# Fused attention and two-layer feed-forward on Trainium2: two more row tiles of w_out ahead of the second half of batch 1's x, and its transpositions in two groups

## The chip, the core and the metric

The kernel runs on one core of one Trainium2 chip. The metric is the device time of one execution in microseconds (us). The kernel before took 202.01 us, the median of 3 runs (201.93 to 202.19).

The engines are named as in the profile: PE (TensorE, matrix products), PEld (its weight loads), DVE (VectorE), ACT (ScalarE), POOL (GpSimd) and SP (SyncE, which here only issues DMAs). L1010 is line 1010 of the kernel.

## What is computed

Eight batches; each has eight heads of a 512 x 64 token matrix x and a 32 x 64 state. Both read each other by softmax attention, the two results are put one above the other (544 rows a batch), and the rows go through two layers with a leaky ReLU between them.

```python
B, H, S, Ns, D = (8, 8, 512, 32, 64)
scale = 1.0 / np.sqrt(D)
scores = scale * np.matmul(x, state.transpose(0, 1, 3, 2))
scores = scores - scores.max(-1, keepdims=True)
a = np.exp(scores)
a /= a.sum(-1, keepdims=True) + 1e-09
xread = np.matmul(a, state)
scores2 = scale * np.matmul(state, x.transpose(0, 1, 3, 2))
...
sread = np.matmul(a2, x)
attn_out = np.concatenate([xread, sread], axis=2)
x = attn_out.transpose(0, 2, 1, 3).reshape(B * S, H * D)
h = x @ w_in
g = np.maximum(0.01 * h, h)
return g @ w_out
```

## The kernel before

**Tiling.** Products take bf16 operands. w_in lies in SBUF as `w_in_bf` (4 blocks of 128 rows), w_out as `w_out_bf` (16 row tiles of 128 x 512). For each batch b an object `a0`, `a1`, `a2`, ... holds the attention's tiles. The first layer is folded with the state: `a_m` (L409) makes a quarter of M = state x w_in (8 small products into PSUM), `m_evict` (L429) copies it to SBUF, and `ff1` (L439) multiplies M by the probabilities `aT` into a bank named ph and applies the leaky ReLU on ACT into `hT`, one of 16 steps of 128 hidden units.

**Batch 0's second layer** is plain: `piece(b, hT, i, jq, js)` (L541) multiplies, for the token block i (four of 128 tokens), the hidden tiles 4 jq + js with the row tiles of w_out of the same numbers into a bank named py or pyw, one product of 128 x 512 each. `half` is `(range(0, 2), range(2, 4))`, so a piece with `half[0]` has two products.

**The order is written by hand**: each engine runs its instructions in the order of the program (`manual_schedule`, L51), and what an instruction waits for is put in as semaphores. The stretch that the change touches stands at L994 to L1037, between batch 0's first layer and batch 1's. In it, in the program's order:

- DVE casts the two halves of batch 1's x, `x1[0]` and `x1[1]` (heads 0 to 3 and 4 to 7, loaded as fp32), to bf16 tiles xb (L995), clears two columns of `stf` (L999), and SP issues eight small loads of the states of batches 2 and 3 into it (`load_state(0)`, L1000, L203).
- ACT makes batch 0's second softmax (`a_exp2`, L347). PE runs the pieces of the row tiles 0 and 1 (L1007, L1009).
- PE transposes batch 1's x by products with the identity, 8 for each half, into a PSUM tile pxt2 of the ring ph (L1015); DVE copies each to `a1.xT` (L1018). The profile prints pxt2 as pxt.
- PE runs the pieces of the row tiles 2 and 3 for token blocks 2 and 3 (L1020), then `a_scores(a1)` (L252: 8 products of the state with xT into sc) and `a_m(a1, 1)` with its copies on ACT (L1022), then the same row tiles for blocks 0 and 1 (L1024).
- DVE finishes batch 0's second softmax (`a_probs2`, L354), then batch 1's first: `a_shift` (row maxima L266, their spread L274, the difference L280) and `a_max2` (L341). POOL starts on sums of blocks of w_out, `tw_sum` (L577), which write over the buffers of x1 and xf.
- PE goes on with row tiles 4 to 7 (L1032), `a_m(a1, 2)` (L1033) and the rest of batch 0's second layer up to row tile 13 (L1036 to L1054). ACT takes the exponential (`a_exp`, L284), copies M (L1035), casts the two halves of batch 2's x (L1041) and makes `a_exp2(a1)` (L1044). SP transposes each half of batch 2's x by DMA (`a_xt_half`, L240). DVE closes the softmax (`a_recip`, `a_probs`: L289 to L302) with aT of batch 1.
- POOL scales the states of batches 2 and 3 (`state_cast(0)`, L209), SP transposes them by DMA into `st_t` (`state_t(0)`, L214) and loads batch 3's x (L1049).
- From L1066 on, `ff1(a1, h1, s)` and the last pieces of batch 0 run in turn; after step 4 come `a_scores(a2)` (L1077), which reads st_t and batch 2's xT.

**The loads** of weights and x up to batch 2 are issued by POOL at L871 to L885 in the order w_in (4), w_out rows 0-1, x1[0], x1[1], rows 2-3, rows 4-7, rows 8-11, first half of batch 2's x, rows 12-13, its second half, rows 14-15. They take eight semaphores in turn, so the ninth load waits on POOL until the first has landed, the tenth for the second, and so on.

Of the kernel before, what the change touches and what calls it, by code (L numbers as in the profile page):

```python
# [9 lines left out]
P = 128  # L10
B, H, S, D = 8, 8, 512, 64
# [4 lines left out]
NT = S // P  # L16
NK = H // 2
SCALE = 1.0 / (D ** 0.5)

BF16 = mybir.dt.bfloat16  # L20
# [7 lines left out]
def kernel(  # L28
# [9 lines left out]
    nc = tc.nc  # L38
# [8 lines left out]
    psum = ctx.enter_context(tc.tile_pool(name="psum", bufs=2, space=bass.MemoryType.PSUM))  # L47
# [5 lines left out]
    VEC, SCA, POO = nc.vector.tensor_copy, nc.scalar.copy, nc.gpsimd.tensor_copy  # L53
# [18 lines left out]
    ident = consts.tile([P, P], BF16, name="ident")  # L72
# [47 lines left out]
    def pair_of(a, t, k):  # L120
        h = 2 * (k % 2)
        return a.xb[k // 2][:, t, h:h + 2, :].rearrange("p h d -> p (h d)")
# [27 lines left out]
    def load_w_out_rows(j0, j1):  # L150
        nc.gpsimd.dma_start(
            w_out_bf[:, j0:j1, :], moe_w_out[P * j0:P * j1, :].rearrange("(j p) f -> p j f", p=P)
        )

    def load_w_out(c):
        load_w_out_rows(4 * c, 4 * (c + 1))
# [39 lines left out]
    stf = [consts.tile([P, hi - lo, P], FP32, name=f"stf{lo}") for lo, hi in groups]  # L196
    stb = [consts.tile([P, hi - lo, P], BF16, name=f"stb{lo}") for lo, hi in groups]

    def load_state(i):
        lo, hi = groups[i]  # L200
        for k in range(NK):
            for g in range(2):
                nc.sync.dma_start(  # L203
                    stf[i][NS * k:NS * (k + 1), :, D * g:D * (g + 1)],
                    state[lo:hi, 2 * k + g].rearrange("b n d -> n b d"),
                )
# [38 lines left out]
    def st_of(a, g, k):  # L245
        rows = slice(D * g, D * (g + 1))
        if a.b == 0:
            return stbd[rows, k, g ^ (k // 2), :]
        t = st1 if a.b == 1 else st_t[0][:, a.b - 2] if a.b < 4 else st_t[1][:, a.b - 4]
        return t[rows, NS * k:NS * (k + 1)]  # L250

    def a_scores(a):  # L252
        sc = psum.tile([P, 2, S], FP32, name="sc", tag="sc", bufs=1)
        for k in range(NK):
            for g in range(2):
                nc.tensor.matmul(  # L256
                    sc[NS * k:NS * (k + 1), g, :],
                    lhsT=st_of(a, g, k),
                    rhs=a.xTh[k // 2][D * g:D * (g + 1), :, k % 2, :],
                    start=True, stop=True,  # L260
                )
        a.sc = sc
# [52 lines left out]
    def a_shift(a):  # L315
        a_max(a)
        a_diff(a)
# [21 lines left out]
    def a_max2(a):  # L339
        a.m2 = att.tile([P, 2], FP32, name="mcol", tag="mcol")  # L340
        nc.vector.tensor_reduce(out=a.m2[:], in_=a.sc[:], axis=AX.X, op=ALU.max, negate=True)  # L341

    def a_exp2(a, g):
        if g == 0:
            a.e2 = att.tile([P, 2, S], BF16, name="e2", tag="e2")
            a.r2 = att.tile([P, 2], FP32, name="r2", tag="r2")
        nc.scalar.activation(  # L347
            out=a.e2[:, g], in_=a.sc[:, g, :], func=AF.Exp,
            bias=a.m2[:, g:g + 1], accum_out=a.r2[:, g:g + 1],
        )  # L350
# [3 lines left out]
    def a_probs2(a):  # L354
        nc.vector.tensor_scalar(out=a.r2[:], in0=a.r2[:], scalar1=1e-9, scalar2=None, op0=ALU.add)
        q2 = att.tile([P, 2], FP32, name="qc", tag="qc")
        nc.vector.reciprocal(q2[:], a.r2[:])
        if a.b in (0, 6):
            pairs[a.b] = att.tile([P, 2, 2, S], BF16, name="a2p", tag="a2p", bufs=1)
        if a.b in (0, 1, 6, 7):  # L360
            a.a2 = pairs[a.b - a.b % 2][:, a.b % 2]
        else:
            a.a2 = att.tile([P, 2, S], BF16, name="a2", tag="a2", bufs=1)[:]
        for g in range(2):
            nc.vector.tensor_scalar(
                out=a.a2[:, g, :], in0=a.e2[:, g, :],
                scalar1=q2[:, g:g + 1], scalar2=None, op0=ALU.mult,
            )
# [40 lines left out]
    def a_m(a, c, tag):  # L409
        if not hasattr(a, "M"):  # L410
            a.M = mpool.tile([P, 2, DFF], BF16, name="M", tag="M")
        if tag in ("ph", "py", "phpy"):
            pm = [psum.tile([P, DM], FP32, name="pm", tag=t) for t in (tag[:2], tag[-2:])]
            at = [t[:] for t in pm]
        else:
            pm = psum.tile([P, 2, DM], FP32, name="pm", tag=tag, bufs=1)
            at = [pm[:, g, :] for g in range(2)]
        for k in range(NK):
            for g in range(2):
                v, r = (k // 2, 2 * (k % 2) + (g ^ (k // 2))) if a.b == 0 else (g, k)  # L420
                nc.tensor.matmul(  # L421
                    at[v][NS * r:NS * (r + 1)],
                    lhsT=st_of(a, g, k),
                    rhs=w_in_bf[D * g:D * (g + 1), k, DM * c:DM * (c + 1)],
                    start=True, stop=True,
                )
        return pm

    def m_evict(a, c, pm, copy):  # L429
        cols = slice(DM * c, DM * (c + 1))  # L430
        if isinstance(pm, list):
            for g in range(2):
                copy(a.M[:, g, cols], pm[g][:])
        else:
            copy(a.M[:, :, cols], pm[:])  # L435
# [105 lines left out]
    def piece(b, hT, i, jq, bank=None, copy=SCA, js=range(4)):  # L541
        if jq == 0 and js[0] == 0:
            y = ys[b, i] = Y()
            y.py = psum.tile([P, DM], FP32, name="py", tag="py")[:] if bank is None else bank
        y = ys[b, i]
        for j in [4 * jq + v for v in js]:
            nc.tensor.matmul(  # L547
                y.py, lhsT=hT[:, j, P * i:P * (i + 1)], rhs=w_out_bf[:, j, :],
                start=(j == 0), stop=(j == 15),
            )  # L550
        if jq == 3 and copy is not None:
            y_store(b, i, copy)

    def y_store(b, i, copy):
        tag = ("ysb", "s1", "ysb", "s6")[i]
        ysb = ypool.tile([P, DM], FP32, name="ysb", tag=tag, bufs=3 if tag == "ysb" else 1)
        copy(ysb[:], ys[b, i].py)
        nc.sync.dma_start(rows_of(b)[i], ysb[:])
# [213 lines left out]
    a0, a1, a2 = att_of[:3]  # L772
# [102 lines left out]
    for u in range(2):  # L875
        nc.gpsimd.dma_start(
            x1[u][:], x[1, NK * u:NK * (u + 1)].rearrange("h (p t) d -> p h (t d)", t=NT)
        )
    load_w_out_rows(2, 4)
    load_w_out(1)  # L880
    load_w_out(2)
    load_x_half(2, 0)
    load_w_out_rows(12, 14)
# [52 lines left out]
    h0 = hpool.tile([P, 16, S], BF16, name="hT", tag="hT")  # L936

    def open_ff1_0(tag):
        if tag in ("sc", "big"):
            pr = psum.tile([P, 2, S], FP32, name="php", tag=tag, bufs=1)  # L940
            return pr, [pr[:, 0], pr[:, 1]]
        ph = [psum.tile([P, S], FP32, name="ph", tag=tag) for _ in range(2)]
        return ph, [p[:] for p in ph]
# [39 lines left out]
    for j, tag in ((4, "ph"), (6, "big"), (8, "py"), (10, "big"), (12, "py"), (14, "ph")):  # L983
        t, bk = open_ff1_0(tag)
# [5 lines left out]
        elif j == 8:  # L990
            a_scores(a0)
            m_halves(a0, 3, "ph")
            a_max2(a0)
    for u in range(2):  # L994
        VEC(  # L995
            a1.xb[u].rearrange("p t h d -> p h t d"),
            x1[u][:].rearrange("p h (t d) -> p h t d", t=NT),
        )
    nc.vector.memset(stf[0][:, 0, D - 1:D + 1], 0.0)  # L999
    load_state(0)  # L1000

    for g in range(2):
        a_exp2(a0, g)
    wide = psum.tile([P, 2, DM], FP32, name="pyw", tag="big", bufs=1)
    half = (range(0, 2), range(2, 4))
    for u in range(2):
        piece(0, h0, 2 + u, 0, bank=wide[:, u], js=half[0])  # L1007
    for i in (0, 1):
        piece(0, h0, i, 0, js=half[0])  # L1009
    for u in range(2):  # L1010
        ps = psum.tile([P, NT, 2, P], BF16, name="pxt2", tag="ph")
        for t in range(NT):
            for v in range(2):
                h = NK * u + 2 * v
                nc.tensor.transpose(  # L1015
                    ps[:, t, v, :], pair_of(a1, t, h // 2), ident[:]
                )
        VEC(a1.xT[:, :, 2 * u:2 * u + 2, :], ps[:])  # L1018
    for i in (2, 3):
        piece(0, h0, i, 0, js=half[1])  # L1020
    a_scores(a1)
    m_evict(a1, 1, a_m(a1, 1, "ph"), SCA)  # L1022
    for i in (0, 1):
        piece(0, h0, i, 0, js=half[1])  # L1024
    a_probs2(a0)
    a_shift(a1)
    a_max2(a1)
    tw_open()
    for j in (4, 6, 0, 2):
        tw_sum(1, j, j + 2, nc.gpsimd)  # L1030
    for i in (0, 1):
        piece(0, h0, i, 1)  # L1032
    pm = a_m(a1, 2, "ph")  # L1033
    a_exp(a1)
    m_evict(a1, 2, pm, SCA)  # L1035
# [93 lines left out]
    for b in range(2, B):  # L1129
# [22 lines left out]
        for s in range(16):  # L1152
# [75 lines left out]
            if b == 7 and s in FA_AT:  # L1228
                i = FA_AT.index(s)
# [49 lines left out]
    for n in (1, 2, 6, 5, 7, 3, 4):  # L1279
        two_product(q, n)  # L1280
        if n in (3, 4):
            u = n - 3
# [43 lines left out]
```

## Time and profile before

| | before |
|---|---|
| median of 3 runs | 202.01 us (201.93 to 202.19) |
| the profiled execution | 202.76 us |
| its span from first to last instruction | 201.0 us |
| granted clock of PE | 1.00 |
| PE busy, share of the span | 97% |
| DVE, ACT, POOL busy | 79%, 71%, 36% |

The profile and every view of the trace show that one profiled execution, with times from the start of its span. A timeline row gives the start, the duration, the engine, the line, the operation, what it writes and reads, and how many instructions are merged; in brackets stands the time the engine sat idle before it and what ended that. The chain of waits is the path that ended last, followed back from the end; its rows give start, duration, engine, tile and line.

### The profile page before, as it was taken

The page shows a single profiled execution, that of the slowest core. Times are in us where ns is not written, and L with a number is a line of the kernel's source. Part 1 is how long each engine was busy: PE and PEld are TensorE (multiplying, and loading weights), DVE is VectorE, ACT ScalarE, POOL GpSimd, SP SyncE. Part 2 cuts the span into 40 slices and gives each one's busy share as a digit, 9 for nine tenths or more (in the row PEclk, how much of TensorE's full clock was granted, in tenths as well). Part 3 has the DMA queues.
Part 4 walks back from the last instruction along what each step waited for, and adds up shares of the span by engine and source line. Part 5 has one row for each costly group of instructions (what it writes and reads, how often), then busy time and mean ns, then how long its engine had stood idle before and what let it go on. Part 6 is the DMA issues. An engine that isn't in the chain of part 4 may idle for free.

```text
span 201.0 us, 4628 instructions
## 1 busy us (share of the span) xinstructions
PE 195.4 (97%) x1880; PEld 130.1 (65%) x1880; DVE 158.7 (79%) x241; ACT 141.9 (71%) x274; POOL 72.6 (36%) x76
## 2 busy tenths in 40 slices
PE   7998999999999999999999999999999999999993
PEld 3643534443476767776776677676767777799982
DVE  3665799399999989985999889898999945984712
ACT  3678738899889868766887779777868555757420
POOL 8823272992091373037300760054004600540000
PEclk9999999999999999999999999999999999999999
DMA  6999998697999944852473404220025302210115
GB/s 198 207 207 297 212 290 147 119 346 170 196 219 228 308 49 72 237 216 55 88 225 139 128 16 92 104 109 0 0 104 157 58 0 104 108 49 8 52 38 170
DMA packets 38773, 27.75 MB, mean 138 GB/s; under 512 B 24416, under 2 KB 35808, under 8 KB 38752
## 3 DMA queue, kind: packets, MB, share of 16 engines
q1 hardware_dynamic: 33584, 20.78, 39.3%
q0 software_dynamic: 4832, 6.29, 15.4%
q10 hardware_dynamic: 336, 0.39, 0.8%
q8 instruction: 14, 0.23, 0.5%
q14 instruction: 7, 0.06, 0.1%
HBM read 17.30 MB, written 8.91 MB: 130 GB/s over the span
## 4 chain that ended last, share of the span: by engine, by line
PE 91%; DMA 3%; DVE 2%; ACT 1%; ACTq 1%; SPq 0%; issue 0%
PE ph L442 24%; PE ppx L642 18%; PE ppb L642 15%; PE py L547 7%; PE ppr L699 6%; PE pm L421 4%; PE pyw L547 3%; PE pf L520 3%; PE ppw L642 3%; DMA xf<-in_x_dram 2%; PE psr L394 2%; PE php L947 1%; PE ph L947 1%; PE sc L256 1%; DMA out_dram<-ysb 1%; DVE m L830 1%
## 5 line engine op out<-in xcount | busy, mean ns | idle before, releaser
L447 ACT ACTIVATE hT<-ph 128x512 bf16<-128x512 f32 x112 | 66.7, 605 | 25.2 <-PE ph L442 24.5
L442 PE MATMUL ph<-aT,M 128*128 128x512 bf16 x224 | 65.5, 380 | 0.0
L607 POOL TENSOR_TENSOR S<-hT,S 128x512 bf16<-128x512 bf16 x24 | 32.1, 1357 | 82.2 <-DVE S L607 55.5
L642 PEld LDWEIGHTS <-S 128*128 128x128 bf16 x384 | 37.0, 98 | 12.7 <-issue 0.9
L642 PEld LDWEIGHTS <-hT 128*128 128x128 bf16 x288 | 28.0, 98 | 11.1
L607 DVE TENSOR_TENSOR S<-hT 128x1024 bf16<-128x1024 bf16 x24 | 25.0, 1069 | 3.3 <-ACT hT L447 3.3
L442 PEld LDWEIGHTS <-M 128*128 128x128 bf16 x224 | 20.9, 98 | 8.8 <-issue 2.9
L642 PE MATMUL ppx<-tw,S 128*128 128x256 bf16 x160 | 20.8, 273 | 0.0
L547 PEld LDWEIGHTS <-hT 128*128 128x128 bf16 x96 | 9.1, 98 | 11.4 <-issue 1.0
L547 PE MATMUL py<-w_out_bf,hT 128*128 128x512 bf16 x64 | 16.0, 380 | 0.0
L739 DVE TENSOR_TENSOR ysb<-ppb,s 128x512 f32<-128x512 f32 x12 | 8.3, 692 | 6.2 <-PE ppb L642 6.1
L642 PE MATMUL ppb<-tw,S 128*128 128x256 bf16 x96 | 12.4, 273 | 0.0
L642 PE MATMUL ppb<-w_out_bf,hT 128*128 128x256 bf16 x96 | 12.4, 273 | 0.0
L642 PE MATMUL ppb<-w_out_bf,S 128*128 128x256 bf16 x96 | 12.3, 273 | 0.0
L435 ACT CAST M<-pm 128x1024 bf16<-128x1024 f32 x11 | 11.2, 1018 | 0.3 <-PE pm L421 0.3
L642 PE MATMUL ppx<-w_out_bf,hT 128*128 128x256 bf16 x80 | 11.2, 273 | 0.0
L347 ACT ACTIVATE e<-sc,mcol 128x512 bf16<-128x512 f32 x16 | 11.1, 700 | 0.0
L586 POOL TENSOR_TENSOR tw<-w_out_bf 128x512 bf16<-128x512 bf16 x8 | 9.0, 1153 | 4.2 <-DMA w_out_bf<-in_moe_w_out_dram 4.2
L642 PE MATMUL ppx<-tw,hT 128*128 128x256 bf16 x80 | 10.4, 273 | 0.0
L341 DVE TENSOR_REDUCE mcol<-sc 128x2 f32<-128x1024 f32 x8 | 9.7, 1214 | 0.0
L266 DVE TRANSPOSE_TENSOR_REDUCE mrow<-sc 128x32 f32<-128x1024 f32 x7 | 8.7, 1242 | 1.2 <-PE sc L256 1.2
L132 POOL CAST xb<-xl 128x2048 bf16<-128x2048 f32 x5 | 9.5, 1892 | 0.0
(148 smaller groups left out, 322.5 us busy)
## 6 DMA issues: line engine op xcount, KB each, us to landing
out_dram<-ysb SPq DMA_DIRECT2D x11, 512.0 KB, 2.6
xl<-in_x_dram SPq DMA_DIRECT2D x5, 1024.0 KB, 6.4
out_dram<-ysb SPq DMA_DIRECT2D x9, 256.0 KB, 4.7
w_in_bf<-in_moe_w_in_dram POOLq DMA_DIRECT2D x4, 512.0 KB, 9.8
xf<-in_x_dram SPq DMA_DIRECT2D x4, 256.0 KB, 3.7
w_out_bf<-in_moe_w_out_dram POOLq DMA_DIRECT2D x4, 256.0 KB, 13.6
x<-in_x_dram POOLq DMA_DIRECT2D x2, 512.0 KB, 14.6
w_out_bf<-in_moe_w_out_dram POOLq DMA_DIRECT2D x2, 512.0 KB, 16.5
```

The source lines that it names most:

```text
L132: nc.gpsimd.tensor_copy(xt[b][:].rearrange("p t h d -> p h t d"), xl[b][:].rearrange("p h (t d) -> p h t d", t=NT),)
L266: nc.vector.tensor_reduce(out=m1[:], in_=flat.rearrange("p (c j) -> p c j", j=NS), axis=AX.X, op=ALU.max, apply_transpose=True,)
L341: nc.vector.tensor_reduce(out=a.m2[:], in_=a.sc[:], axis=AX.X, op=ALU.max, negate=True)
L347: nc.scalar.activation(out=a.e2[:, g], in_=a.sc[:, g, :], func=AF.Exp, bias=a.m2[:, g:g + 1], accum_out=a.r2[:, g:g + 1],)
L435: copy(a.M[:, :, cols], pm[:])
L442: nc.tensor.matmul(ph[:], lhsT=a.M[:, g, P * j:P * (j + 1)], rhs=a.aT[:, g, :], start=(g == 0), stop=(g == 1),)
L447: nc.scalar.activation(out=hT[:, j, :], in_=ph[:], func=AF.Prelu, scale=1 / SCALE, alpha=0.01)
L547: nc.tensor.matmul(y.py, lhsT=hT[:, j, P * i:P * (i + 1)], rhs=w_out_bf[:, j, :], start=(j == 0), stop=(j == 15),)
L586: eng.tensor_tensor(out=tw[n][u][:, at], in0=in0, in1=in1, op=ALU.subtract)
L607: eng.tensor_tensor(out=part(n), in0=in0, in1=in1, op=op)
L642: nc.tensor.matmul(q[bank][v], lhsT=lhsT, rhs=w_of(n, j), start=q["open", bank] and j == 0, stop=j == 7, skip_group_check=True,)
L699: nc.tensor.matmul(q.bank[w], lhsT=lhsT, rhs=w_of(n, j), start=n in (1, 2, 5) and j == 0, stop=j == HJ - 1, skip_group_check=True,)
```

## The change

The loads of x1 and w_out are interleaved: row tiles 2-3 now stand ahead of x1[1], and the load of rows 4-7 becomes two, 4-5 and 6-7, of which both stand behind x1[1]. The casts, transpositions and copies of batch 1's x are done half by half: the first half as before; between its transpositions and those of the second half PE runs the pieces of row tiles 2 and 3 for all four token blocks. The second half's cast, `a_probs2(a0)` and its copy follow in this order on DVE. The pieces of row tiles 4 and 5 for blocks 0 and 1 now stand ahead of `a_scores(a1)`, those of 6 and 7 behind `a_m(a1, 1)`. The memset of stf and `load_state(0)` come behind the first copy.

```diff
@@ -876,8 +876,8 @@
         nc.gpsimd.dma_start(
             x1[u][:], x[1, NK * u:NK * (u + 1)].rearrange("h (p t) d -> p h (t d)", t=NT)
         )
-    load_w_out_rows(2, 4)
-    load_w_out(1)
+        load_w_out_rows(2 + 2 * u, 4 + 2 * u)
+    load_w_out_rows(6, 8)
     load_w_out(2)
     load_x_half(2, 0)
     load_w_out_rows(12, 14)
@@ -991,14 +991,26 @@
             a_scores(a0)
             m_halves(a0, 3, "ph")
             a_max2(a0)
-    for u in range(2):
+    def x1_cast(u):
         VEC(
             a1.xb[u].rearrange("p t h d -> p h t d"),
             x1[u][:].rearrange("p h (t d) -> p h t d", t=NT),
         )
-    nc.vector.memset(stf[0][:, 0, D - 1:D + 1], 0.0)
-    load_state(0)
-
+
+    def x1_t(u):
+        ps = psum.tile([P, NT, 2, P], BF16, name="pxt2", tag="ph")
+        for t in range(NT):
+            for v in range(2):
+                h = NK * u + 2 * v
+                nc.tensor.transpose(
+                    ps[:, t, v, :], pair_of(a1, t, h // 2), ident[:]
+                )
+        return ps
+
+    def x1_copy(u, ps):
+        VEC(a1.xT[:, :, 2 * u:2 * u + 2, :], ps[:])
+
+    x1_cast(0)
     for g in range(2):
         a_exp2(a0, g)
     wide = psum.tile([P, 2, DM], FP32, name="pyw", tag="big", bufs=1)
@@ -1007,29 +1019,25 @@
         piece(0, h0, 2 + u, 0, bank=wide[:, u], js=half[0])
     for i in (0, 1):
         piece(0, h0, i, 0, js=half[0])
-    for u in range(2):
-        ps = psum.tile([P, NT, 2, P], BF16, name="pxt2", tag="ph")
-        for t in range(NT):
-            for v in range(2):
-                h = NK * u + 2 * v
-                nc.tensor.transpose(
-                    ps[:, t, v, :], pair_of(a1, t, h // 2), ident[:]
-                )
-        VEC(a1.xT[:, :, 2 * u:2 * u + 2, :], ps[:])
-    for i in (2, 3):
+    x1_copy(0, x1_t(0))
+    nc.vector.memset(stf[0][:, 0, D - 1:D + 1], 0.0)
+    load_state(0)
+    x1_cast(1)
+    a_probs2(a0)
+    for i in (2, 3, 0, 1):
         piece(0, h0, i, 0, js=half[1])
+    x1_copy(1, x1_t(1))
+    for i in (0, 1):
+        piece(0, h0, i, 1, js=half[0])
     a_scores(a1)
     m_evict(a1, 1, a_m(a1, 1, "ph"), SCA)
-    for i in (0, 1):
-        piece(0, h0, i, 0, js=half[1])
-    a_probs2(a0)
     a_shift(a1)
     a_max2(a1)
     tw_open()
     for j in (4, 6, 0, 2):
         tw_sum(1, j, j + 2, nc.gpsimd)
     for i in (0, 1):
-        piece(0, h0, i, 1)
+        piece(0, h0, i, 1, js=half[1])
     pm = a_m(a1, 2, "ph")
     a_exp(a1)
     m_evict(a1, 2, pm, SCA)
```

## The prediction

> **What bounds the kernel now.** I read the page first, then the chain of waits, then each engine's timeline between 20 and 40 us. The page's shares of the chain that ended last:
>
> ```profile
> PE 91%; DMA 3%; DVE 2%; ACT 1%; ACTq 1%; SPq 0%; issue 0%
> ```
>
> PE is the path, so a change counts as far as it adds or takes away waits of PE. The chain of waits through the changed stretch, from batch 1's transpositions on (start, duration):
>
> ```profile
> 23.19 0.89 PE pxt L1015 x16
> 24.09 0.86 PE pyw L547 x4
> 24.95 0.47 PE sc L256 x8
> 25.41 0.22 PE pm L421 x8
> 25.63 2.69 PE py L547 x12
> 28.33 0.34 PE pm L421 x8
> 28.67 1.83 PE pyw L547 x8
> 30.50 1.73 PE py L547 x8
> 32.23 2.59 PE pyw L547 x12
> 34.82 0.86 PE py L547 x4
> ...
> 39.57 0.34 PE sc L256 x8
> 39.91 0.22 PE pm L421 x8
> ```
>
> All of it is PE, piece on piece. The one wait that I find is in the scores of batch 1: 0.47 us, where batch 2's, just as long and standing behind full products too, take 0.34. So **0.13 us** is all that this trace offers. The next views are the rows of DVE and, last, the first product of batch 1's first layer on PE:
>
> ```profile
> 21.27 0.69 DVE L995 CAST xb<-x 128x1024 bf16<-128x1024 f32 x1
> 22.52 0.69 DVE L995 CAST xb<-x 128x1024 bf16<-128x1024 f32 x1 [0.56 <-DMA x<-in_x_dram]
> ...
> 23.68 1.29 DVE L1018 COPY xT<-pxt 128x1024 bf16<-128x1024 bf16 x2 [0.45 <-PE pxt L1015]
> 24.88 0.16 DVE L355 TENSOR_SCALAR r<-r 128x2 f32<-128x2 f32 x1
> ...
> 25.28 0.62 DVE L365 TENSOR_SCALAR a2p<-e,qc 128x512 bf16<-128x512 bf16 x2
> 25.81 1.24 DVE L266 TRANSPOSE_TENSOR_REDUCE mrow<-sc 128x32 f32<-128x1024 f32 x1
> ...
> 33.87 0.69 DVE L302 TENSOR_TENSOR aT<-e,qb 128x1024 bf16<-128x1024 bf16 x1
> ...
> 39.98 1.25 DVE L266 TRANSPOSE_TENSOR_REDUCE mrow<-sc 128x32 f32<-128x1024 f32 x1 [1.22 <-PE sc L256]
> ```
> ```profile
> 35.52 1.03 PE L442 MATMUL ph<-aT,M 128*128 128x512 bf16 x4
> ```
>
> DVE is a chain of its own here: from the row maxima (25.81) to the end of aT (33.87 + 0.69 = 34.56) it is 8.75 us, one operation behind the other. PE takes up aT at 35.52, so this chain has 0.96 us in hand.
>
> **PE's own work.** The number of products does not change. After the change, from 23.19 on, with the rows above: 8 transpositions (half of 0.89) to 23.64; 8 products of row tiles 2 and 3 (2 x 0.86) to 25.36; 8 transpositions to 25.81; 4 products of row tiles 4 and 5 to 26.67; scores without a wait, 0.34, to 27.01; a_m 0.22 to 27.23; 4 products 0.86, and 0.10 more behind small products (the 12 take 2.69, three times 0.86 is 2.58), to 28.19; a_m 0.34 to 28.53; then 1.83 + 1.73 + 2.59 + 0.86 = 7.01 to 35.54. Before, that point is 35.68. By work alone PE would gain 0.14.
>
> The operands are there. The casts' row shows x1[1] landing at 22.52; loads run in order, and from the landing of rows 2-3 below one load is about 1.1, so it lands at 23.6. DVE takes it up only behind the first copy (half of 1.29 from 23.68, to 24.4), ends the cast at 25.1 and a_probs2 (24.88 to 25.90 now, 1.02) at 26.1. PE's second transpositions start at 25.36, after the cast. The second copy then ends near 26.7, where PE wants it: nothing, at most 0.1.
>
> **A new wait on ACT.** The change leaves 4 products between the two a_m, where there were 12. The two banks of the ring ph must be copied out between:
>
> ```profile
> 25.67 1.07 ACT L433 CAST M<-pm 128x512 bf16<-128x512 f32 x2 [1.59 <-PE pm L421]
> ...
> 29.62 1.06 ACT L284 ACTIVATE e<-sh 128x1024 bf16<-128x1024 f32 x1 [2.88 <-DVE sh L280]
> ...
> 31.52 1.06 ACT L126 CAST xb<-xl 128x1024 bf16<-128x1024 f32 x1
> 33.41 1.04 ACT L126 CAST xb<-xl 128x1024 bf16<-128x1024 f32 x1 [0.83 <-DMA xl<-in_x_dram]
> ```
>
> The copies end 1.11 after a_m (26.74 against 25.63), so at 28.34; PE comes at 28.19. That is 0.15 to 0.2, and PE reaches batch 1's first layer at 35.5 to 35.7, about as before.
>
> **The softmax starts later.** This decides. Before, the scores ended at 25.41, and DVE took them up at 25.81, when a_probs2 was done. Now they end at 27.01; batch 2's maxima start 0.07 after their scores (39.91 to 39.98), so these start at 27.08, **1.27 later**. The exponential on ACT lies beside batch 1's second maximum on DVE, so nothing in the 8.75 us gives way: aT ends at 35.83. With some 0.05 for the hand-over the first layer starts at 35.88 instead of 35.52: **+0.36 us**, in which the gain and the ACT wait above are swallowed. Everything that PE does later moves with it.
>
> **Behind the exponential.** Its start (29.62) moves by the same 1.27, and with it ACT's M copies and the cast of batch 2's first half. SP waits for that cast:
>
> ```profile
> 23.27 3.63 SPq L203 DMA_DIRECT2D stf<-in_state_dram  x8
> ```
> ```profile
> 32.60 2.05 SPq L240 DMA_TRANSPOSE xT<-xb  x1
> ```
> ```profile
> 34.76 1.24 SPq L240 DMA_TRANSPOSE xT<-xb  x1
> 36.10 1.19 SPq L214 DMA_TRANSPOSE st_t<-stb  x1
> ```
> ```profile
> st_t<-stb SPq DMA_TRANSPOSE x1, 2.9
> ```
> ```profile
> 39.49 0.11 PEld L256 LDWEIGHTS <-st_t 64*32 64x32 bf16 x8 [0.42 <-DMA st_t<-stb]
> ```
> ```profile
> L372 SPq DMA_TRANSPOSE a2T<-a x4: 1232/1270/2805, 54.4 to 110.8; - x4
> ```
>
> The first cast ends at 32.58 and SP issues at 32.60, so now at 33.87. The second cast, which waited for its load at 33.41, now runs from 33.85 to 34.9 and is no later than its turn on SP. With the durations of these rows (2.16 to the next issue, 1.34 to the one behind it) st_t is issued at 37.37 and lands 2.9 later, at 40.3; before, 36.10 + 2.9 = 39.0. PE loads it at 39.49 now and would come at 39.85: a **second wait of about 0.45 us**, to 40.3. What is uncertain is the issue of 2.05: the next one, as large, took 1.24, and the row of a2T, also as large, spans 1.23 to 2.81. With 1.24, st_t lands at 39.5 and the wait is gone; with 2.81 it grows by 0.76. I take 2.05, since it is the same instruction's own row.
>
> The eight loads of stf start behind the first copy, at 24.4 instead of 23.27, and their 3.63 us end at 28.1, well ahead of 33.87. The scaling on POOL, which waits for them, then has until 37.37. Batch 3's x, behind st_t on SP, moves by 1.27 as well; I cost it at nothing, since its first products come in b = 2, and at up to 0.9 (1.27 less 0.36) if that cover is gone. POOL's tw sums can start earlier, as row tiles 4 and 5 land sooner; nothing but batch 2's products reads them.
>
> Sum: 0.36 + 0.45 = 0.81 us against the profiled execution (span 201.0, time 202.76). I add it to the median, 202.01, as it stands: **202.8 us**.
>
> **The rivals.**
>
> *Only the first wait*: the issue of xT takes 1.24 to 1.6. 202.01 + 0.36 = 202.4, on the bound of what a measurement can tell from no change (0.2%, 0.4 us). For it: the second xT issue took 1.24, and half of the a2T row 1.27 or less. Against it: the instruction's own 2.05. A long one, 2.81, makes 203.6.
>
> *The loads are later in the timed runs than in the profiled one, and the sum ends at no change or below.* The place is PE's first use of x1[1] and of row tiles 2 and 3. The POOL rows and two times to landing:
>
> ```profile
> 8.31 0.75 POOL L151 DMA_DIRECT2D w_out_bf<-in_moe_w_out_dram  x1
> ...
> 12.40 0.74 POOL L151 DMA_DIRECT2D w_out_bf<-in_moe_w_out_dram  x1 [1.77 <-DMA w_in_bf<-in_moe_w_in_dram]
> 16.10 0.76 POOL L106 DMA_DIRECT2D xl<-in_x_dram  x1 [2.96 <-DMA w_in_bf<-in_moe_w_in_dram]
> ```
> ```profile
> w_out_bf<-in_moe_w_out_dram POOLq DMA_DIRECT2D x1, 256.0 KB, 15.3
> ```
> ```profile
> w_out_bf<-in_moe_w_out_dram POOLq DMA_DIRECT2D x1, 512.0 KB, 16.7
> ```
>
> Rows 2-3 land at 8.31 + 15.3 = 23.6 and are used at about 24; the second cast ends at 23.21 and its transpositions start near 23.5. So before has only some 0.2 to 0.3 in hand. After the change it is 0.8: x1[1] at 23.6 against 24.4 on DVE, and row tiles 4 and 5 (23.6 + 1.3) against 25.81. If the loads are late by L, before loses L - 0.2 and the changed kernel nothing up to 0.8, so the change wins back at most 0.6: 201.8 if st_t does not wait, 202.2 if it does. It decides from L = 0.56 on. For it: the timed runs are 0.75 us shorter than the profiled one. Against it: PE has no wait for a load in this stretch.
>
> *The split load holds up all the loads behind it.* POOL waits for the eighth load before, so with one load more, rows 8-11 go out at 16.10, in the slot of the next load, not at 12.40. If a load always took its 16.7 us, they would land at 32.8 instead of 29.1; PE wants them at 30.5, waits 2.3 us and reaches the first layer at 37.8: 202.01 + 2.2 = 204.2. Against it: x1[1] and rows 2-3, issued in turn, land 1.1 us apart, each after 15 us, so the time is spent in a queue that stays full, and a later place in POOL's order does not move a landing. The Trainium skill ("DMA: Bandwidth & Descriptors", section "Anatomy of one DMA — SWDGE (gpsimd) path") gives each such DMA a fixed cost of about 2.0 us, mostly its completion, beside its bytes; added to every load behind, rows 8-11 would come at an estimated 31.1 and the sum would be near 203. The spacing of 1.1 us, under that fixed cost, speaks against adding it.
>
> *Neither wait comes*: if DVE's chain were 0.36 shorter and st_t in time, PE keeps its 0.14, 201.9. No row of the chain shows a gap to close.
>
> **How the numbers follow.** Both waits as priced, 0.42: slower. Only the first, 0.26, divided by the bound: 0.09 slower, 0.17 the same. A longer issue, 0.05: slower. Late loads, 0.18: 0.11 the same, 0.07 faster (where the last rival comes with it: 201.9 - 0.6 = 201.3). The split, 0.04: slower. Neither wait, 0.05: 0.03 the same, 0.02 faster. That is slower 0.60, the same 0.31, faster 0.09. The range of 201.8 to 203.2 takes in the first two cases and most of the late loads and leaves out 203.6, 204.2 and the faster end, 0.18 in all.
>
> **What would show it.** In the changed trace: the row maxima of batch 1 near 27.1, aT ending near 35.8, PE's first ph<-aT,M at 35.9 behind a gap of 0.2 to 0.5; the xT issue on SP near 33.9; the weight load of st_t near 40.3 behind a wait for its DMA; the second a_m of batch 1 behind ACT. Landings of rows 8-11 and of batch 2's x unmoved. It is wrong if the maxima start before 26.5, if st_t lands before 39.9 (then 202.4), or if a wait of PE for a load that the profile hides was there before.

## The result, and the profile after

The changed kernel took **204.84 us** (median of 6 runs), the kernel before, on the same chip, 202.22 us (6 runs). One disturbed run of the changed kernel (207.36 us) is left out of the ratio; the median of the five others is 204.30. The ratio is 1.012, with a 95% interval of 1.0083 to 1.0157: slower by 1.7 to 3.2 us, where the forecast was 202.8 and its range ended at 203.2. The profiled execution took 205.61 us with a span of 203.8, against 201.0 before, and the granted clock was 1.00 in both, so the two traces can be laid side by side. It is the longest of the five (204.14 to 205.61), so what its trace shows as lost lies above the 2.4 us of the ratio.

The shares of the chain that ended last, from the page of the changed kernel:

```profile
PE 74%; DVE 16%; ACT 3%; DMA 3%; issue 2%; ACTq 1%
```

Before, it was PE 91% and DVE 2%. Where DVE came onto the path is seen in the chain of waits of the changed kernel, from batch 1's transpositions on (start, duration):

```profile
23.11 0.46 PE pxt L1005 x8
...
23.60 0.69 DVE xT L1011
...
24.82 1.13 DVE r L355
...
26.17 2.16 DVE a2p L365 x2
...
28.33 0.61 DVE xT L1011
...
28.98 0.42 PE sc L256 x4
...
29.43 1.26 DVE mrow L266
...
37.50 0.70 DVE aT L302
38.20 0.05 issue
38.24 0.62 PE ph L442 x2
```

The chain leaves PE at 23.60 and comes back to it for good only at 38.24, with the first product of batch 1's first layer. The waits of PE between 20 and 60 us, all of them (who waited, for whom, us in total, times, the longest):

```profile
PE sc L256 <- DVE xT L1011: 2.1, 1, 2.1
PE py L547 <- issue: 0.2, 1, 0.2
```

So PE waits in the scores of batch 1 for the second copy of xT, which I had costed at nothing, at most 0.1. None of its waits is for a load or for st_t. DVE's timeline shows why the copy is late:

```profile
24.21 0.69 DVE L995 CAST xb<-x 128x1024 bf16<-128x1024 f32 x1
...
24.82 1.12 DVE L355 TENSOR_SCALAR r<-r 128x2 f32<-128x2 f32 x1
25.97 0.17 DVE L357 RECIPROCAL qc<-r 128x2 f32<-128x2 f32 x1
26.17 2.16 DVE L365 TENSOR_SCALAR a2p<-e,qc 128x512 bf16<-128x512 bf16 x2
28.25 0.68 DVE L1011 COPY xT<-pxt 128x1024 bf16<-128x1024 bf16 x1
29.43 1.25 DVE L266 TRANSPOSE_TENSOR_REDUCE mrow<-sc 128x32 f32<-128x1024 f32 x1 [0.50 <-PE sc L256]
```

No row of a_probs2 has a bracket: DVE waits for nothing there. But the same instructions have become longer. The 128x2 L355 takes 1.12 instead of 0.16, the two L365 2.16 instead of 0.62, a_probs2 as a whole 3.5 instead of 1.0. The reciprocal between them still takes 0.17. What else had changed at that time stands in POOL's timeline; before:

```profile
26.29 4.50 POOL L586 TENSOR_TENSOR tw<-w_out_bf 128x512 bf16<-128x512 bf16 x4 [4.18 <-DMA w_out_bf<-in_moe_w_out_dram]
```

and after, where the first, the second with the third, and the fourth of these sums are shown apart:

```profile
24.23 1.68 POOL L586 TENSOR_TENSOR tw<-w_out_bf 128x512 bf16<-128x512 bf16 x1 [1.67 <-DMA w_out_bf<-in_moe_w_out_dram]
...
25.88 2.30 POOL L586 TENSOR_TENSOR tw<-w_out_bf 128x512 bf16<-128x512 bf16 x2
...
28.14 1.20 POOL L586 TENSOR_TENSOR tw<-w_out_bf 128x512 bf16<-128x512 bf16 x1
```

The first sum reads row tiles 4 and 5 and waits for their load. Before, that load brought 4 to 7, and the sum started at 26.29, behind a_probs2 (which ended at 25.28 + 0.62 = 25.90). Now it starts 2.06 us earlier, at 24.23, ahead of a_probs2. And the ends agree: the first sum ends at 24.23 + 1.68 = 25.91 and L355 at 24.82 + 1.12 = 25.94; the third ends at 25.88 + 2.30 = 28.18 and the second L365 at 26.17 + 2.16 = 28.33.

**Theory 1.** A DVE operation of certain kinds that reads SBUF (tensor_scalar and cast among them) and a POOL sum that reads SBUF do not run beside each other: the one that comes second stands still until the first is done, and the time is put down to it as duration. L355 and the two L365 each stand behind a sum that was there first. The second copy, behind them in DVE's order, PE's scores, the maxima and the softmax chain are late by that.

**The rivals**: the two engines share a bandwidth, so that each gets slower in proportion to what it moves; the new order of PE, or the later start of the softmax, costs the time and the long L355 and L365 only fill a wait; the new order of the loads costs it, by what then lands late.

### The profile page after: what moved, and what is told of

The parts are those of the page before. It is cut to its first block, busy times and chain, and to the rows that moved or that the text cites. A ratio compares the mean times of both kernels' runs of the same rounds, so it can differ in the third digit from the quotient of the medians.

```text
span 203.8 us, 4603 instructions
## 1 busy us (share of the span) xinstructions
PE 195.1 (96%) x1853; PEld 130.8 (64%) x1880; DVE 161.6 (79%) x241; ACT 142.0 (70%) x274; POOL 73.6 (36%) x77
## 4 chain that ended last, share of the span: by engine, by line
PE 74%; DVE 16%; ACT 3%; DMA 3%; issue 2%; ACTq 1%
PE ph L442 18%; PE ppx L642 18%; PE ppb L642 15%; PE ppr L699 5%; PE pf L520 3%; PE pm L421 3%; PE ppw L642 3%; PE ph L947 2%; DVE sh L274 2%; PE psr L394 2%; DVE mrow L266 2%; DMA xf<-in_x_dram 2%; DVE a2p L365 1%; DVE qb L298 1%; DVE r L289 1%
## 5 line engine op out<-in xcount | busy, mean ns | idle before, releaser
L442 PE MATMUL ph<-aT,M 128*128 128x512 bf16 x202 | 60.9, 379 | 0.2
L642 PE MATMUL ppb<-w_out_bf,S 128*128 128x256 bf16 x96 | 12.3, 273 | 0.1
L586 POOL TENSOR_TENSOR tw<-w_out_bf 128x512 bf16<-128x512 bf16 x8 | 9.6, 1228 | 1.7 <-DMA w_out_bf<-in_moe_w_out_dram 1.7
```

Source lines behind the costliest of these rows:

```text
L442: nc.tensor.matmul(ph[:], lhsT=a.M[:, g, P * j:P * (j + 1)], rhs=a.aT[:, g, :], start=(g == 0), stop=(g == 1),)
L586: eng.tensor_tensor(out=tw[n][u][:, at], in0=in0, in1=in1, op=ALU.subtract)
L642: nc.tensor.matmul(q[bank][v], lhsT=lhsT, rhs=w_of(n, j), start=q["open", bank] and j == 0, stop=j == 7, skip_group_check=True,)
```

## The experiments

The traces differ by about 1 us in when batch 1's transpositions start: 22.18 to 23.03 us in the kernel before and those made from it, 22.44 to 23.24 in the changed one and those made from it. So in each profiled run I count from PE's first transposition of batch 1 (pxt): to the first product ph<-aT,M of batch 1's first layer, and to the end of the span. Before, these are 35.52 - 23.03 = 12.49 and 201.0 - 23.03 = 177.97. The table gives what is added to them, and the measured ratio to the kernel before, which was run beside it. The ratio comes from all the runs, the last two columns from one profiled run each.

| kernel | median, us (runs) | ratio, 95% interval | first layer | end |
|---|---|---|---|---|
| changed kernel | 204.84 (6) | 1.012, 1.0083 to 1.0157 | +2.80 | +2.88 |
| e1: changed, POOL held | 202.72 (12) | 1.0024, 1.0013 to 1.0035 | +0.39 | +0.49 |
| e2: before, new loads alone | 204.20 (4) | 1.009, 1.0077 to 1.0103 | +2.06 | +2.15 |
| e3: changed, old loads | 203.66 (5) | 1.0059, 1.0046 to 1.0072 | +0.55 | +0.69 |
| e4: changed, a_probs2 later | 203.79 (6) | 1.0087, 1.0061 to 1.0114 | +0.40 | +1.48 |
| e5: before, three more sums on POOL | 203.44 (9) | 1.0065, 1.0043 to 1.0088 | +1.34 | +1.49 |
| e7: changed, L365's scalings on ACT | 202.97 (12) | 1.0035, 1.0009 to 1.0061 | +1.59 | +1.69 |
| e8: changed, POOL's sums halved | 204.18 (7) | 1.0071, 1.004 to 1.0102 | +1.36 | +1.45 |
| e9: before, PE's two groups alone | 203.57 (6) | 1.0057, 1.0038 to 1.0075 | +1.16 | +1.23 |
| e10: e9, POOL held | 202.76 (12) | 1.0019, 1.0006 to 1.0033 | -0.09 | +0.08 |
| e11: before, POOL held | 202.18 (11) | 0.9995, 0.9983 to 1.0008 | 0.00 | -0.01 |

### e1: POOL held back in the changed kernel

A small copy on POOL reads batch 1's row maxima, so the sums behind it start when a_probs2 is long done. All else is the change.

```diff
+    held = att.tile([P, NB], FP32, name="held", tag="held", bufs=1)
+    nc.gpsimd.tensor_copy(held[:], a1.m1[:])
     for j in (4, 6, 0, 2):
         tw_sum(1, j, j + 2, nc.gpsimd)
```

> The changed kernel, with POOL's first sums of w_out held back until batch 1's row maxima are done (a 128 x 32 copy on POOL that reads them stands ahead of the sums). Theory 1 (POOL's sums, which now start at 24.2 us, hold up DVE's a_probs2): a_probs2 takes 1.0 us again instead of 3.5, the row maxima start near 27.1, the first layer of batch 1 near 35.9, and the time is 0.3 to 0.9 us over before. Rival A (the split load and the slots of the load queue make the loads late) and rival B (the order of PE's work alone): the row maxima stay near 29.4 and the time 2 to 3 us over before.

DVE's rows and POOL's:

```profile
24.31 0.16 DVE L355 TENSOR_SCALAR r<-r 128x2 f32<-128x2 f32 x1
...
24.70 0.61 DVE L365 TENSOR_SCALAR a2p<-e,qc 128x512 bf16<-128x512 bf16 x2
...
26.50 1.25 DVE L266 TRANSPOSE_TENSOR_REDUCE mrow<-sc 128x32 f32<-128x1024 f32 x1 [0.55 <-PE sc L256]
```
```profile
28.06 4.50 POOL L586 TENSOR_TENSOR tw<-w_out_bf 128x512 bf16<-128x512 bf16 x4
```

a_probs2 is back at 1.0 us. The maxima come 26.50 - 22.44 = 4.06 behind the first transposition (6.48 in the changed kernel), and of +2.80 at the first layer +0.39 is left. The ratio goes down from 1.012 to 1.0024, by some 1.9 us. Most of the loss is the collision; what is left is the size of the first wait that I had forecast.

### e2 and e3: the loads alone, the order alone

e2 is the kernel before with the first hunk of the change only:

```diff
-    load_w_out_rows(2, 4)
-    load_w_out(1)
+        load_w_out_rows(2 + 2 * u, 4 + 2 * u)
+    load_w_out_rows(6, 8)
```

> The kernel before, with the new order of the loads alone. Theory 1: POOL's sums start near 24.2 instead of 26.3, while DVE is at a_probs2 (24.9 to 25.9), which grows by 1.5 to 2.5 us; the row maxima start near 28, and since aT has 0.96 us in hand, the time is 0.7 to 1.8 us over before. Rival A: 2 us or more over before, with a wait of PE for a load. Rival B: within 0.5 us of before, with the row maxima at most 1 us later, since x1's second half lands 1 us later.

```profile
25.12 0.35 DVE L355 TENSOR_SCALAR r<-r 128x2 f32<-128x2 f32 x1
...
25.72 2.28 DVE L365 TENSOR_SCALAR a2p<-e,qc 128x512 bf16<-128x512 bf16 x2
```
```profile
24.30 4.71 POOL L586 TENSOR_TENSOR tw<-w_out_bf 128x512 bf16<-128x512 bf16 x4 [1.66 <-DMA w_out_bf<-in_moe_w_out_dram]
```

The loads alone bring the collision: the sums start at 24.30, a_probs2 takes 2.9. PE also waits 1.07 at its second group of transpositions, whose x lands later now and, without the new order, is wanted at once. The maxima come 27.92 - 22.18 = 5.74 behind the first transposition instead of 2.78: of these 2.96 us, 1.9 are a_probs2 and 1.1 the later x, which by itself would have used up little more than the 0.96 in hand. 1.009 (+1.8 us) is at the upper end of what theory 1 had expected.

e3 is the changed kernel with that hunk taken back.

> The changed kernel, with the loads as before. Theory 1: rows 4-7 land near 26.1, so the sums start when a_probs2 is over and it stays at 1.0 us; PE waits some 0.4 us for these rows ahead of the scores, the maxima start near 27.5, and the time is 0.5 to 1.3 us over before. Rival A: no slower than before by over 0.4. Rival B: 2 to 3 us over before.

```profile
25.50 0.62 DVE L365 TENSOR_SCALAR a2p<-e,qc 128x512 bf16<-128x512 bf16 x2
```
```profile
26.14 4.49 POOL L586 TENSOR_TENSOR tw<-w_out_bf 128x512 bf16<-128x512 bf16 x4 [4.22 <-DVE a2p L365]
```

The two L365 take 0.62 and POOL's sums start at 26.14, behind them by 0.02 (25.50 + 0.62 = 26.12 is the end of the second). The profiled run loses 0.55 at the first layer. The ratio, 1.0059 or +1.2 us, is in the expected span, but the profiled run shows only 0.69 of it. With 0.02 us between a_probs2 and the sums, other runs may well fall into the collision; or this kernel's transpositions start later as a rule (23.24 here, the latest of all), which the count from them leaves out. Only one run has a trace, so this stays open.

### e4: a_probs2 behind the softmax of batch 1

```diff
-    a_probs2(a0)
     for i in (2, 3, 0, 1):
         piece(0, h0, i, 0, js=half[1])
```

and `a_probs2(a0)` again behind `a_probs(a1)`; POOL's sums are as early as in the changed kernel (24.25).

> The changed kernel, with a_probs2 of batch 0 behind batch 1's a_probs on DVE, where POOL's first sums are over. Theory 1: DVE's second copy of xT follows its cast, the row maxima start near 27.0 though POOL's sums still start at 24.2, a_probs2 takes 1.0 us at its new place, and the time is 0.3 to 0.9 us over before. Rival A and rival B: the row maxima are late by what they were, the time 2 to 3 us over before.

```profile
26.51 1.25 DVE L266 TRANSPOSE_TENSOR_REDUCE mrow<-sc 128x32 f32<-128x1024 f32 x1 [0.55 <-PE sc L256]
```

Up to the first layer it went as expected: the maxima are where e1 has them, +0.40, although POOL is at its sums all the time. The total missed, by about 0.9. It is lost in batch 2's softmax, at another meeting of the same sort, DVE's L293 and POOL's cast of batch 3's x:

```profile
46.59 1.50 DVE L293 TENSOR_SCALAR r<-r 128x32 f32<-128x32 f32 x1
```
```profile
46.17 1.88 POOL L132 CAST xb<-xl 128x2048 bf16<-128x2048 f32 x1
```
```profile
53.53 0.41 PE L256 MATMUL sc<-xT,st_t 64*32 64x512 bf16 x8 [0.65 <-DVE M L435]
```

L293 takes 0.18 where it is alone. Here it ends 0.04 behind POOL's cast (46.59 + 1.50 = 48.09; 46.17 + 1.88 = 48.05). Moving DVE's work had moved POOL's stream, which waits for a sum of DVE's, by 1 us (the cast starts at 45.22 in e1), and the cast into L293's way. The before kernel escapes it by 0.2 (46.76 on DVE, 44.65 + 1.89 = 46.54 on POOL); in the changed kernel and the other experiments but e11 L293 takes some 0.57, and there the last column of the table stands 0.07 to 0.17 above the one beside it.

### e5: the collision brought into the kernel before

The order and loads of before, and three more sums on POOL as soon as row tiles 2 and 3 are there; their output is overwritten later.

```diff
+    for _ in range(3):
+        with nc.allow_low_precision(reason="operands of bf16 products"):
+            nc.gpsimd.tensor_tensor(
+                out=tw[3][0][:, 0:2], in0=w_block(0, 1, 2, 4), in1=w_block(0, 0, 2, 4),
+                op=ALU.subtract,
+            )
```

> The kernel before, with three more sums on POOL ahead of its own (operands: row tiles 2-3, landed at 23.6 us; their output is written over later). Loads and order are those of before. Theory 1 (a POOL operation under way holds up a DVE tensor_scalar that reads SBUF): POOL is busy from 23.7 us, a_probs2 of batch 0 grows from 1.0 us by 1.5 to 2.5 us, the row maxima start near 28, and after the 0.96 us that aT has in hand the time is 0.7 to 1.8 us over before. If the order or the loads were the cause: as before, within 0.3 us.

```profile
24.31 0.44 DVE L355 TENSOR_SCALAR r<-r 128x2 f32<-128x2 f32 x1
...
24.99 2.35 DVE L365 TENSOR_SCALAR a2p<-e,qc 128x512 bf16<-128x512 bf16 x2
```

The same long rows and 1.0065 (+1.3 us), with nothing of the change in the kernel. PE's first product of the layer has `0.91 <-DVE aT L302` ahead of it: the maxima come 27.26 - 22.24 = 5.02 behind the first transposition instead of 25.81 - 23.03 = 2.78. That is 2.24 later, 0.96 of it was in hand, and the rest, 1.28, is nearly the +1.34 of the table.

### e6: the operations by themselves, beside POOL

A kernel of its own, which leaves out the whole computation: each of eight DVE operations three times alone, then three times beside six POOL sums of two 128x512 bf16 tiles.

```python
for _ in range(3):
    case()
...
for i in range(6):
    nc.gpsimd.tensor_tensor(out=z[i % 2][:], in0=w[:, 0], in1=w[:, 1], op=ALU.subtract)
...
for _ in range(3):
    case()
```

> A kernel of its own that leaves out the whole computation: eight DVE operations of this kernel, each three times with POOL idle and three times beside a train of six POOL tensor_tensor of 128x512 bf16. Theory 1: the tensor_scalar of 128x2 and of 128x512 and the cast from SBUF wait for the end of the POOL operation under way, so some 1.1 us each however small; reads of PSUM, the reciprocal, and the spread keep their time. The product of two SBUF tiles is open. Theory 2 (DVE and POOL share a bandwidth): all that touch SBUF grow by a like factor, the 128x2 one by next to nothing.

For each operation the first row is alone and the second beside POOL (the duration is that of three):

```profile
5.38 0.57 DVE L58 TENSOR_SCALAR os<-r 128x2 f32<-128x2 f32 x3
...
6.46 3.33 DVE L58 TENSOR_SCALAR os<-r 128x2 f32<-128x2 f32 x3
...
13.73 1.12 DVE L61 TENSOR_SCALAR ob<-w,r 128x512 bf16<-128x512 bf16 x3
...
16.30 3.60 DVE L61 TENSOR_SCALAR ob<-w,r 128x512 bf16<-128x512 bf16 x3
...
22.65 0.56 DVE L64 RECIPROCAL os<-r 128x2 f32<-128x2 f32 x3
...
24.65 0.55 DVE L64 RECIPROCAL os<-r 128x2 f32<-128x2 f32 x3
...
42.00 3.73 DVE L70 CAST ob<-pp 128x1024 bf16<-128x1024 f32 x3
...
47.18 3.73 DVE L70 CAST ob<-pp 128x1024 bf16<-128x1024 f32 x3
...
64.83 1.33 DVE L79 TENSOR_TENSOR ob<-w 128x512 bf16<-128x512 bf16 x3
...
67.61 4.00 DVE L79 TENSOR_TENSOR ob<-w 128x512 bf16<-128x512 bf16 x3
```

A tensor_scalar of 128x2 is held as long as one of 128x512: by 0.92 and 0.83 us each, where one POOL sum takes 1.1 (six in 6.73). A bandwidth that is split would cost the small one next to nothing. The reciprocal and the cast that reads PSUM aren't touched; nor are the transposing maxima from PSUM (3.81 and 3.80) and the spread by stream transposition (3.80 and 3.79). The cast that reads SBUF goes from 2.14 to 4.80 and a product of two SBUF tiles from 1.33 to 4.00. It agrees with the changed kernel, where L355 and L365 grew, and the reciprocal and the copy from PSUM beside the sums did not, and with e4, where the maxima beside them took their 1.25.

The Trainium skill states this rule ("SBUF — State Buffer", section "Who interferes with whom"): DVE and GpSimd share one pair of SBUF ports, which is an exclusive lock; whichever starts first holds it for its whole instruction and the other one is blocked. It names copy, cast and tensor_scalar in their two-port modes, and operations with two SBUF inputs against a GpSimd operation that reads SBUF. The traces agree: 0.57 to 3.33 and 1.33 to 4.00 for three, 3.73 unchanged from PSUM. With it and the sums' earlier start, the prediction could have found the collision.

### e7: the scalings of a_probs2 on ACT

```diff
-    a_probs2(a0)
...
+    for g in range(2):
+        nc.scalar.activation(
+            out=a0.a2[:, g, :], in_=a0.e2[:, g, :], func=AF.Copy, scale=q20[:, g:g + 1]
+        )
```

Its sum with 1e-9 and reciprocal stay on DVE, at lines 1026 and 1028.

> The changed kernel, with the two scalings of batch 0's second softmax (L365) on ACT instead of DVE; POOL's sums still start near 24.2 us. Theory 1: only the small tensor_scalar (L355) still waits, up to 1.1 us, and the second copy of xT starts by 26.2; the row maxima start at 27.0 to 27.4 and the time is 0.4 to 1.0 us over before. If the loads were the cause, 2 us over before as in the changed kernel.

```profile
24.21 1.67 DVE L995 CAST xb<-x 128x1024 bf16<-128x1024 f32 x1
...
25.80 1.11 DVE L1026 TENSOR_SCALAR r<-r 128x2 f32<-128x2 f32 x1
```

In the timed runs it met the expectation: 1.0035, +0.7 us, where the changed kernel loses 2.4. In the profiled run the gain is smaller, since there POOL's first sum came ahead of the second cast, which took 1.67 instead of 0.69 and held PE up by 0.66. In the changed kernel's own run the cast started 0.02 ahead of the sum and it was the sum that waited. So which of the two comes first differs between these two traces, by a few hundredths of a us. Three of e7's twelve runs, the profiled one among them, took 204.3 to 204.5 us and the nine others 202.7 to 203.3; the order of cast and sum would explain that, but only one run has a trace.

### e8: POOL's sums cut in two

```diff
-    for j in (4, 6, 0, 2):
-        tw_sum(1, j, j + 2, nc.gpsimd)
+    for j in (4, 5, 6, 7, 0, 1, 2, 3):
+        tw_sum(1, j, j + 1, nc.gpsimd)
```

> The changed kernel, with POOL's first sums cut into eight of one row tile each. Theory 1: a DVE operation waits for the end of one POOL operation, now some 0.6 us instead of 1.15, so a_probs2 takes 1.8 to 2.4 us instead of 3.5, and the time falls to 1.0 to 1.8 us over before. Theory 2 (shared bandwidth): no change against the changed kernel, since POOL is as busy.

```profile
24.94 0.63 DVE L355 TENSOR_SCALAR r<-r 128x2 f32<-128x2 f32 x1
...
25.81 1.20 DVE L365 TENSOR_SCALAR a2p<-e,qc 128x512 bf16<-128x512 bf16 x2
```

POOL moves the same bytes in nearly the same stretch (5.69 us against 5.11), in sums half as long, and each DVE operation waits about half as long: a_probs2 takes 2.1 instead of 3.5, and PE's wait in the scores goes from 2.06 to 0.61. A split bandwidth would have left these as they were. That rival falls.

### e9, e10 and e11: the two groups without the loads, and the hold by itself

e9 is the kernel before with PE's order alone: pieces between the two groups of transpositions, with the loads, the casts and a_probs2 where they were.

```diff
         VEC(a1.xT[:, :, 2 * u:2 * u + 2, :], ps[:])
-    for i in (2, 3):
+        if u == 0:
+            for i in (2, 3):
+                piece(0, h0, i, 0, js=half[1])
+    for i in (0, 1):
         piece(0, h0, i, 0, js=half[1])
     a_scores(a1)
     m_evict(a1, 1, a_m(a1, 1, "ph"), SCA)
-    for i in (0, 1):
-        piece(0, h0, i, 0, js=half[1])
```

> The kernel before, with only PE's order changed: the four products of row tiles 2 and 3 for blocks 2 and 3 stand between the two groups of transpositions, those for blocks 0 and 1 ahead of the scores. Loads and DVE's order stay. Theory 1 and the working by PE's rows: the wait of 0.13 us in the scores goes, the row maxima start at most 0.2 us later, POOL's sums do not meet a_probs2, and the time is 0 to 0.2 us under before. If two groups as such cost time: 0.3 us or more over before.

This one missed: 1.0057, +1.15 us, where I had expected no loss. The rows of e9:

```profile
25.50 0.16 DVE L355 TENSOR_SCALAR r<-r 128x2 f32<-128x2 f32 x1
...
25.89 1.52 DVE L365 TENSOR_SCALAR a2p<-e,qc 128x512 bf16<-128x512 bf16 x2
```
```profile
26.07 4.58 POOL L586 TENSOR_TENSOR tw<-w_out_bf 128x512 bf16<-128x512 bf16 x4 [4.08 <-DMA w_out_bf<-in_moe_w_out_dram]
```

The second copy, and a_probs2 behind it, come later in DVE's order, and the loads of before are early enough for POOL to catch L365 there. So the kernel before ends a_probs2 only 0.4 us ahead of the sums (25.90 and 26.29), and either half of the change is enough to use that up. Whether the rest of e9's loss is the order itself, e10 tells: e9 with the copy of e1 ahead of the sums. e11 is the kernel before with that copy, as a control on the hold.

> The kernel of the run before with PE's two groups alone, and the small copy on POOL that holds its sums of w_out back until batch 1's row maxima. Theory 1 (what that run lost was L365 caught by POOL's first sum): both scalings take 0.62 us again, the maxima start at once behind them, 3.9 us after the first transposition weight load (4.83 without the hold, 2.78 in the kernel before), which uses up the 0.96 us that DVE's chain had in hand and 0.2 more: PE waits 0.2 us for aT in place of 0.69, and the time is 0.2 to 0.5 us above before, where it was 1.15 above. Rival (the order by itself costs PE a us, by its extra waits for row tiles 2 and 3 and for the second copy): the time stays 0.9 to 1.3 us above before, although L365 takes 0.62.

> The kernel before, with nothing but the small copy on POOL that holds its sums back until batch 1's row maxima: a control on what the hold does by itself. Before's sums start 0.4 us behind the end of a_probs2, so there is no collision to take away, and they then start some 0.9 us later. Theory 1: within 0.2 us of before, the maxima and PE's first product of batch 1's layer where they were. Rival (the hold itself saves or costs time elsewhere, by moving POOL's sums against other work of DVE, so that the held kernels' gains are not the collision's): 0.4 us or more either way.

```profile
25.91 0.62 DVE L365 TENSOR_SCALAR a2p<-e,qc 128x512 bf16<-128x512 bf16 x2
```

That is e10's row. Its ratio is 1.0019 (+0.4 us): of e9's 1.15 the hold takes away some 0.75. The profiled run is better than expected (-0.09 at the first layer), since PE had no wait for row tiles 2 and 3 in it, as it had in e9's (0.28). e11 is at 0.9995: holding POOL back neither saves nor costs a time that can be told from nothing where there is no collision (-0.3 to +0.2 us). The gains of e1 and e10 are the collision's.

## Why the prediction was wrong, point by point

- **The failed step** is the last sentence on the parts of the change: "POOL's tw sums can start earlier, as row tiles 4 and 5 land sooner; nothing but batch 2's products reads them." I asked who reads the sums, and not whom they disturb while they run. The step was costed at 0. It took 2.80 - 0.39 = 2.41 us at the first layer (the changed kernel against e1), and some 1.9 in the timed runs (1.012 against 1.0024). None of the rivals had it either.
- **The second copy and a_probs2**: I took a_probs2's 1.02 from before, where it ran with POOL idle (POOL's sums came 0.4 us behind it). The duration of a row holds only with the neighbours that it had.
- **The first wait was right.** Forecast were the maxima at 27.08, 4.05 behind the first transposition, and 0.36 at the first layer. With POOL held (e1), they are 4.06 and 0.39, and the time is 1.0013 to 1.0035, that is +0.3 to +0.7 us. That the gain on PE and the wait for ACT are swallowed by it was right too: in e1 aT ends at 34.57 + 0.69 = 35.26, and PE takes it up at 35.32.
- **The second wait did not come.** I had it at 0.45 with 2.05 for SP's first xT issue. SP, and PE's weight load, in the changed kernel:

```profile
36.23 1.32 SPq L240 DMA_TRANSPOSE xT<-xb  x1
...
37.67 1.26 SPq L240 DMA_TRANSPOSE xT<-xb  x1
...
39.04 1.18 SPq L214 DMA_TRANSPOSE st_t<-stb  x1
```
```profile
42.23 0.11 PEld L256 LDWEIGHTS <-st_t 64*32 64x32 bf16 x8 [0.42 <-DMA st_t<-stb]
```

  The issue took 1.32, not 2.05, which is the rival "only the first wait". The 0.42 ahead of the weight load stood there before too, and PE's list of waits has no entry for it. Across the traces the issue takes 2.05 (before) and 2.45 (e11) where it begins while the second half of batch 2's x is still being loaded (ACT waits for that load until 33.41 and 32.84, the issues begin at 32.60 and 31.83), and 1.32 in the changed kernel; in the nine others the two issues together take 2.69 to 2.72, as they do in the changed kernel (2.70; before 3.40, e11 3.79). In the changed kernel and those made from it the issue begins 1.3 us or more later, counted from the first transposition, and ACT no longer waits for that load. That the load is the reason fits all the traces, but no run tested it.
- **The split load held up nothing**: no wait of PE for a load stands in the list above, so that rival was rightly given little. Rows 8-11, issued at 15.64 instead of 12.40, landed 12.3 us later, at 27.9 instead of 29.1 before, and not at the estimated 31.1. Late loads held up PE twice, in kernels with half of the change: 0.28 in e9, and 1.07 in e2 by way of the cast.
- **The sign was right, but for the smaller part of the loss**: the first wait alone would have been 0.39 of 2.80. Of what was to show it, the maxima (27.1 forecast, 29.43 measured) and aT are late by the collision, and the rest moved with them. That the measured time went the forecast way is therefore in the main luck.

No kernel here beats the one before. The best versions with the new order, e1 and e10, are still 0.4 to 0.5 us behind it, as its maxima start later; and the wait that the change could have removed was only 0.13.

## What to carry to other kernels

When a load is made earlier, look at every engine that it releases, and at what the other engines do at that new time: POOL's work that "nobody waits for" can sit on DVE's path without being read by anyone. If a DVE row gets longer with no bracket ahead of it, lay POOL's timeline beside it and see whether the ends agree. To start a POOL stream behind DVE's short SBUF work, one small copy that reads DVE's next result is enough (0.21 us on POOL, here worth some 1.9).

## What the runs showed of the hardware

- The block is not seen as idle time or as a wait but as duration: 0.16 became 1.12 for a 128x2 operation, and PE's wait was put down to the copy behind it in DVE's order, which itself ran at full pace (0.68).
- The price is set by what is left of the other engine's instruction, not by the size of one's own: with POOL's sums half as long (e8) it was about half, 0.63 and 1.20 us in place of 1.12 and 2.16.
- It goes both ways: in the changed kernel POOL's first sum, which started 0.02 us behind DVE's cast, took 1.68, where four alone take 4.50.
- DVE's cast and maxima from PSUM, its reciprocal and its stream transposition ran beside POOL at full pace (e6: 3.73, 3.80, 0.55 and 3.79 us for three, alone 3.73, 3.81, 0.56 and 3.80), so the two engines can share a stretch if DVE's share of it is of these kinds.
